# Turning q and k of steps 0 to 5 in TensorE's transpose mode, with half-size loads and with k and v on GpSimd's queue

## The chip, the cores and the metric

The kernel runs on one core of a Trainium2 chip. A core has TensorE (PE, matrix products), VectorE (DVE), ScalarE (ACT), GpSimd (POOL) and SyncE (SP), which run side by side and wait for each other on semaphores. The metric is the device time of one execution in microseconds (us). A measurement is the median of several executions; a profiled execution gives the trace.

## The reference

The program is a retention block followed by a feed-forward block; q, k, v and the result are float32:

```python
# q, k, v: (B=4, H=8, S=768, D=64)
gamma = 1.0 - 2.0 ** (-5.0 - np.arange(H))
for t in range(S):
    state = gamma[None, :, None, None] * state + np.einsum('bhd,bhe->bhde', k[:, :, t], v[:, :, t])
    y[:, :, t] = scale * np.einsum('bhd,bhde->bhe', q[:, :, t], state)
# y as x: 3072 tokens x 512; w_in is 512 x 2048, w_out 2048 x 512
h = x @ w_in
g = h * (1.0 / (1.0 + np.exp(-1.702 * h)))
out = g @ w_out
```

Both weights are float64 and are narrowed to float32 on the chip.

## The kernel before

**Retention by chunks.** The sequence is cut into chunks of 64 positions. A *step* j handles one chunk of two batches at once, the one in partitions 0 to 63, the other in 64 to 127, for all eight heads; there are 24 steps. A step loads q, k and v (`load`), turns q and k so that the head dimension lies in the partitions (`turn`, then `turned` copies the result out of PSUM), multiplies k by q (`attend`, line 288) and masks the product with the decay (`masked`). One step later it takes the state's update from k and v (line 296), the part of the output from the old state (305) and the part from within the chunk (311). `by_state` and `output` join both parts into X, the input of the feed-forward block; `aged` and `updated` bring the state forward, and `decay` scales k for the update.

Steps 0 to 5 (`j < NEW`) and the later ones differ. The early steps load q, k and v as they lie, one DMA for each batch, and turn q and k on TensorE by a matmul with the identity: 16 matmuls a step, each for one head of both batches, with a result of 64 partitions by 128 (line 249). Head `HP * r + s` goes to partitions 64r to 64r+63 of slot s, where HP is 4. ScalarE copies the result out (260) and scales k (271). From step 6 on, VectorE transposes 32 by 32 blocks (252) that were loaded in many small DMAs.

**Feed-forward.** The first block of four steps is multiplied directly (`up0`, line 413), the second too (`up1`, 426); later blocks use fewer products on sums of sub-blocks (471, 575, 708). The weights come in 512 KB transfers (`fetch`, 178) into three raw buffers in turn and are narrowed by ScalarE (`abs`, 205) and VectorE (`half`: 209 to 211, `rest`: 215 to 220).

**What sets the order.** For the opening, one long list of words written by hand gives the order of the work: `k0` loads k of step 0, `turn2` turns step 2, `w3b` fetches half of a weight panel, `abs3 half3 rest3` narrow panel 3, `up0.0.2` is an up-projection, `step-2` is the later half of step 2 and `step3` the first half of step 3. Each engine and each queue executes its own part of the list in this order, and an instruction that waits holds up all those behind it on its engine. The part around the first steps reads:

```python
k0 table q0 warm turn0 w0b rows warm k1 abs0b q1 turned0 step0 v0 w0a half0b mask turn1 causal rest0b
masked0 decay0 v1 decay1 abs0a half0a step-0 updated0 turned1 q2 step1 rowd k2 whole w2b turn2 w2a x0 k3
aged1 masked1 turned2 v2 rest0a abs2 q3 step-1 updated1 state1 decay2 aged2 step2 q4 x1 half2 decay3 w3b
w3a up0.0.0 masked2 turn3 k4 step-2 v3 q5 rest2 k5 gate0.0.0 turned3 updated2 state2 step3 up0.0.2
```

`mask` is a product on VectorE that waits for `rows` on TensorE; `causal` is GpSimd's part of it (772), two instructions that wait for `mask`. `whole` is a pair of small DMAs (783) with the decay over a chunk, which `aged` reads on ScalarE (356). All q, k and v go by SP's queue, except k of step 0, which goes by ScalarE's. The q and k tiles have two buffers each, and so have the v tiles: the load of step j waits until step j - 2 has been read. GpSimd issues only the small decay tables in the opening. `whole_h` (793) is such a table for the steps after 5; it isn't pinned to its place in the list, and the scheduler put it at the head of GpSimd's queue.

Of the kernel before, what the change touches and what calls it, by code (L numbers as in the profile page):

```python
# [11 lines left out]
AF = mybir.ActivationFunctionType  # L12
ALU = mybir.AluOpType
P = 128
# [14 lines left out]
def kernel(  # L29
# [29 lines left out]
    pe, act, dve, pool, sp = nc.tensor, nc.scalar, nc.vector, nc.gpsimd, nc.sync  # L59
    ctx.enter_context(tc.manual_schedule(engines={mybir.EngineType.PE}))  # L60

    B, H, S, D = q.shape
    NT, DM = out.shape
    DFF = moe_w_in.shape[1]
    HP = H // 2
# [38 lines left out]
    cold = const.tile([P, 2 * H], F32, name="cold")  # L104
    whole = const.tile([P, HP], F32, name="whole")
    whole_h = const.tile([P, H], F32, name="whole_h")
    ident = const.tile([P, P], F32, name="ident")
# [10 lines left out]
    def pin(i):  # L118
        return tc.keep_in_program_order(i) if ordered[0] else i


    NEW = 6
    QKV = {}

    def load(j, what="qkv"):

        b, c = j // NC * 2, j % NC
        rows = slice(c * D, (c + 1) * D)  # L130
        keep = tc.keep_in_program_order if j < 2 * CB else lambda i: i

        def plain(name, src, tag, bufs, engine=sp):
            t = two.tile([P, H, D], F32, name=name + "_in", tag=tag, bufs=bufs)
            QKV[name, j] = t
            for i in range(2):
                if j < NEW:
                    keep(engine.dma_start(t[i * D:(i + 1) * D], src[b + i, :, rows, :].rearrange("h p d -> p h d")))  # L138
                else:
                    for r in range(2):  # L140
                        keep(engine.dma_start(t[r * D:(r + 1) * D, i * HP:(i + 1) * HP],
                                              src[b + i, r * HP:(r + 1) * HP, rows, :].rearrange("h p d -> p h d")))

        if j < NEW:
            if "q" in what:
                plain("q", q, "q_sq", 2)
            if "k" in what:
                plain("kn", k, "k_sq", 2, sp if j else act)
        elif "q" in what:
            for name, src in (("q", q), ("k", k)):  # L150
                t = two.tile([P, H, D // C4, C4], F32, name=name + "_sq")
                for r0 in range(0, P, C4):
                    for n in range(D // C4):
                        t0 = c * D + n * C4
                        tc.keep_in_program_order(sp.dma_start(
                            t[r0:r0 + C4, :, n], src[b + r0 // D, :, t0:t0 + C4, r0 % D:r0 % D + C4]
                            .rearrange("h p d -> p h d")))
                QKV[name, j] = t
        if "v" in what:
            if j >= NEW and c < NC - 1:  # L160
                plain("kn", k, "kn", 1)
            plain("v", v, "v", 2)


    w1v = moe_w_in.bitcast(U32).rearrange("(c p) (f two) -> p c f two", p=P, two=2)
# [59 lines left out]
    QT, KT, KD, AT, TURNED, PA, PU, PY, SHARE = [{} for _ in range(9)]  # L225
    HALF = [slice(i * D, (i + 1) * D) for i in range(2)]
    TWO = [(i, r) for i in range(2) for r in range(2)]

    def home(j, name):

        at = ["qT", "kT", "kd", "at"].index(name)
        shape = [[HP, P] if j < NEW else [H, D]] * 2 + [[H, D], [2, HP, D]]
        shape = shape[at]
        if j >= 2 * CB:
            return one.tile([P] + shape, F32, name=name, tag=name, bufs=[2, 1, 1, 2][at])
        t = G[:, at, j % 2 * 2:j % 2 * 2 + 2].rearrange("p s t -> p (s t)")
        return t.rearrange("p (a b c) -> p a b c", a=2, b=HP) if at == 3 else t.rearrange("p (a b) -> p a b", a=shape[0])

    def turn(j):

        QT[j], KT[j] = home(j, "qT"), home(j, "kT")
        if j < NEW:

            x = QKV.pop(("q", j)), QKV["kn", j]
            TURNED[j] = p = [ps.tile([P, HP, P], F32, name="pt", tag="y") for i in range(2)]
            for n in (1, 0) if j else (0, 1):
                for s in range(HP):
                    for r in range(2):
                        pe.matmul(p[n][HALF[r], s, :], x[n][:, HP * r + s, :], ident, start=True, stop=True)  # L249
        else:  # L250
            for t, name in ((QT[j], "q"), (KT[j], "k")):
                tc.keep_in_program_order(dve.transpose(
                    t.rearrange("p h t -> p (h t)"), QKV.pop((name, j)).rearrange("p h n d -> p (h n d)")))
        if 2 * CB <= j < NCH - 2:
            load(j + 2, "qk")
# [6 lines left out]
    def decay(j):  # L262

        if j % NC == NC - 1:
            return
        KD[j] = home(j, "kd")
        x = QKV["kn", j]
        if j < NEW:

            for h in range(H):  # L270
                pin(act.activation(KD[j][:, h], x[:, h], AF.Copy, scale=cold[:, H + h:H + h + 1]))
        else:
            pool.tensor_mul(KD[j].rearrange("p (i s) d -> p i s d", i=2), x.rearrange("p (i s) d -> p i s d", i=2),
                            cold[:, None, H:H + HP, None].to_broadcast([P, 2, HP, D]))
# [94 lines left out]
    def step(j, f=None):  # L369
        attend(j, f)  # L370
        if j is not None:
            masked(j)
            if j > 2 * CB:
                decay(j)
        if f is not None:
            c = f % NC
            if c == 0:
                updated(f)
            else:
                by_state(f)  # L380
            output(f)
            if 0 < c < NC - 1:
                aged(f)
                updated(f)
        if j is not None and 2 * CB < j < NCH - 1:
            load(j + 1, "v")
# [356 lines left out]
    W = col_decay.shape[1]  # L743
# [43 lines left out]
    def late_loads():  # L787
        load(2 * CB, "qkv")
        load(2 * CB + 1, "qk")

    def halves_anew():

        pool.dma_start(whole_h, bass.AP(tensor=col_decay.tensor, offset=col_decay.offset + (D - 1) * W + H,
                                        ap=[[0, P], [1, H]]))
        pool.tensor_copy(mask[HALF[1], 0], mask[HALF[1], 1])
        pool.tensor_copy(cold[HALF[1], H:H + HP], cold[HALF[1], H + HP:2 * H])
        old, new = state[NEW % NC % 2], state[(NEW + 1) % NC % 2]
        for u in range(2):
            pool.dma_start(new[HALF[1 - u], u], old[HALF[u], 1 - u])
        for u in range(2):  # L800
            pool.tensor_copy(old[HALF[u], 1 - u], new[HALF[u], 1 - u])
# [5 lines left out]
        "mask": lambda: pin(dve.tensor_mul(m3, products["rows"], cold[:, 0:H, None].to_broadcast([P, H, D]))),  # L807
        "causal": causal, "rows": rows,
        "rowd": lay_rowd, "whole": lay_whole, "late_loads": late_loads, "anew": halves_anew,
        "warm": keep_warm}  # L810
    for j in range(2 * CB):
        for name in "qkv":
            works[f"{name}{j}"] = lambda j=j, name=name: load(j, name)
        works |= {f"{name}{j}": lambda j=j, do=do: do(j) for name, do in (
            ("turn", turn), ("turned", turned), ("decay", decay), ("masked", masked), ("state", by_state),
            ("x", output), ("aged", aged), ("updated", updated))}
        for f in (None, *range(2 * CB)):
            works[f"step{j}" + ("" if f is None else f"-{f}")] = lambda j=j, f=f: attend(j, f)
        works[f"step-{j}"] = lambda j=j: attend(None, j)
    for i in range(2 * NFF):  # L820
        works[f"w{i // 2}{'ab'[i % 2]}"] = lambda i=i: fetch(i)
    for name, i in [("0a", 0), ("0b", 1)] + [(str(p), 2 * p) for p in range(1, NFF)]:
        n = Narrow(i)
# [41 lines left out]
    for m in range(NB):  # L865
        between = []
        if m == 0:
            between = [lambda: turn(2 * CB), lambda: step(2 * CB), lambda: None, lambda: None, lambda: turn(2 * CB + 1)]
        elif m == 1:
            between = [lambda: (decay(2 * CB), load(2 * CB + 1, "v"))]  # L870
            for j in range(2 * CB + 1, 3 * CB + 1):
                between.append(lambda j=j: (step(j, j - 1), j < 3 * CB and turn(j + 1)))
        elif 1 < m < NB - 1:
            last = min((m + 2) * CB, NCH - 1)
            for j in range((m + 1) * CB + 1, last + 1):
                between.append(lambda j=j: (step(j, j - 1), j < last and turn(j + 1)))
            if last == NCH - 1:
                between.append(lambda: step(None, NCH - 1))
# [77 lines left out]
```

## Time and profile before

| | |
|---|---|
| median of 8 executions | 667.18 us (665.85 to 668.38) |
| profiled execution | 666.63 us, of it 664.9 us from the first to the last instruction (the span) |
| TensorE busy | 649.2 us (98%) |
| VectorE busy | 435.2 us (65%) |
| ScalarE busy | 148.8 us (22%) |
| GpSimd busy | 176.5 us (27%) |
| mean granted TensorE clock | 0.997 |
| line 249, the turns | 192 records, in steps 0 to 5, between 6.6 and 44 us |

How to read it: the rows overlap, as the engines run side by side. Each float32 matmul leaves two records in the trace, so 192 records are 96 matmuls. In the lists that follow, a line gives the engine, the line of the kernel, what is written and read, and a time; `SPq` and `ACTq` are the queues of DMA issues of those engines, while GpSimd's issues are shown as its own instructions. "<-" names what ended a wait.

### The profile page before, as it was taken

What the parts mean: (1) busy time and instruction counts of PE and PEld (TensorE: products, weight loads), DVE (VectorE), ACT (ScalarE), POOL (GpSimd) and SP (SyncE); (2) the same over time, 40 slices, a digit from 0 to 9 for tenths busy, and PEclk for the clock granted to TensorE, in tenths of its full rate; (3) what the DMA queues carried; (4) which work ended last, traced back from release to release, by engine and by line L of the source; (5) the groups of instructions that cost most, each with busy time, mean ns of one, the idle gap of its engine ahead of it and who ended that gap; (6) DMA issues with size and microseconds to landing.
All of it is one profiled execution on the core that took longest, in us unless ns stands there. A gap on an engine that the chain in (4) does not pass through costs nothing.

```text
span 664.9 us, 15234 instructions
## 1 busy us (share of the span) xinstructions
PE 649.2 (98%) x6438; PEld 564.1 (85%) x6438; DVE 435.2 (65%) x618; ACT 148.8 (22%) x285; POOL 176.5 (27%) x196
## 2 busy tenths in 40 slices
PE   6799999999999999999999999999999999999997
PEld 4688885446888888888999888999888999988997
DVE  3789778798545775456985345995254995254965
ACT  5664222231000000233110234010233110233110
POOL 3000310000278326100446500354700255500000
PEclk9899999999999999999999999999999999999999
DMA  9987647542203546263385742285652243602142
GB/s 182 224 205 207 169 83 230 172 80 36 45 12 132 174 108 185 60 226 123 87 221 131 253 90 95 83 203 145 196 155 96 66 147 109 234 20 95 52 157 95
DMA packets 150500, 89.49 MB, mean 135 GB/s; under 512 B 136192, under 2 KB 137472, under 8 KB 149408
## 3 DMA queue, kind: packets, MB, share of 16 engines
q1 hardware_dynamic: 140944, 46.50, 30.4%
q0 software_dynamic: 7184, 40.78, 16.9%
q10 hardware_dynamic: 2304, 1.25, 0.6%
q8 instruction: 50, 0.82, 0.5%
q14 instruction: 18, 0.15, 0.1%
HBM read 72.89 MB, written 15.47 MB: 133 GB/s over the span
## 4 chain that ended last, share of the span: by engine, by line
PE 88%; DMA 4%; DVE 3%; SPq 2%; POOL 2%; issue 1%; ACT 1%; POOLq 0%; DVEq 0%
PE pq L575 24%; PE px L471 16%; PE pd L708 13%; PE py L471 12%; PE ph L426 8%; PE ph L413 5%; PE pa L288 2%; PE py L311 2%; PE pa L296 2%; PE py L305 1%; DMA kn_in<-in_k_dram 1%; PE pt L249 1%; DMA W<-in_moe_w_out_dram 1%; DMA q_in<-in_q_dram 1%; SPq L138 1%
## 5 line engine op out<-in xcount | busy, mean ns | idle before, releaser
L575 PE MATMUL pq<-W,G 128*128 128x128 f32 x672 | 80.5, 276 | 0.5 <-issue 0.5
L575 PEld LDWEIGHTS pq<-W,G 128*128 128x128 f32 x672 | 77.6, 192 | 1.3 <-issue 0.7
L544 POOL DMA_DIRECT2D ring<-W2D x28 | 15.4, 551 | 228.7 <-PE px L471 118.2
L471 PE MATMUL px<-X,W1A 128*128 128x256 f32 x256 | 60.1, 380 | 0.5 <-POOL X L441 0.5
L471 PE MATMUL px<-X,W1B 128*128 128x256 f32 x256 | 59.8, 379 | 0.0
L575 PE MATMUL pq<-ring,own 128*128 128x128 f32 x448 | 59.8, 277 | 0.0
L575 PEld LDWEIGHTS pq<-ring,own 128*128 128x128 f32 x448 | 54.5, 192 | 0.4
L471 PEld LDWEIGHTS px<-X,W1A 128*128 128x128 f32 x256 | 48.3, 190 | 7.5 <-POOL X L441 1.2
L471 PEld LDWEIGHTS px<-X,W1B 128*128 128x128 f32 x256 | 48.6, 190 | 6.6
L708 PE MATMUL pd<-W,G 128*128 128x256 f32 x224 | 49.6, 381 | 0.0
L708 PEld LDWEIGHTS pd<-W,G 128*128 128x128 f32 x224 | 42.3, 190 | 5.8
L471 PE MATMUL py<-X,W1B 128*128 128x256 f32 x192 | 45.4, 379 | 0.0
L471 PE MATMUL py<-X,W1A 128*128 128x256 f32 x192 | 45.4, 379 | 0.0
L392 ACT ACTIVATE G<-G 128x512 f32<-128x512 f32 x48 | 30.2, 630 | 52.0 <-DVE G L481 33.4
L471 PEld LDWEIGHTS py<-X,W1B 128*128 128x128 f32 x192 | 36.5, 190 | 4.9
L471 PEld LDWEIGHTS py<-X,W1A 128*128 128x128 f32 x192 | 36.5, 190 | 4.9
L489 DVE TENSOR_TENSOR t<-py,u 128x512 f32<-128x512 f32 x16 | 11.1, 692 | 32.9 <-PE py L471 32.9
L478 ACT ACTIVATE p<-px 128x512 f32<-128x512 f32 x16 | 9.6, 597 | 94.3 <-PE px L471 94.3
L575 PE MATMUL pq<-ring,G 128*128 128x128 f32 x224 | 29.6, 275 | 0.0
L575 PE MATMUL pq<-W,own 128*128 128x128 f32 x224 | 29.6, 275 | 0.0
L503 DVE TENSOR_TENSOR G<-G 128x512 f32<-128x512 f32 (+2 forms) x24 | 12.3, 514 | 25.7 <-ACT G L392 25.7
L413 PE MATMUL ph<-X,W1B 128*128 128x256 f32 x128 | 29.0, 383 | 0.0
(206 smaller groups left out, 1165.9 us busy)
## 6 DMA issues: line engine op xcount, KB each, us to landing
ring<-W2D POOLq DMA_DIRECT2D x28, 768.0 KB, 4.9
W1B<-W1D POOLq DMA_DIRECT2D x6, 1792.0 KB, 9.1
W<-in_moe_w_in_dram SPq DMA_DIRECT2D x12, 512.0 KB, 6.1
W<-in_moe_w_out_dram SPq DMA_DIRECT2D x10, 512.0 KB, 4.8
out_dram<-o POOLq DMA_DIRECT2D x20, 256.0 KB, 3.2
q_sq<-in_q_dram SPq DMA_DIRECT2D x144, 32.0 KB, 2.2
k_sq<-in_k_dram SPq DMA_DIRECT2D x144, 32.0 KB, 2.3
v_in<-in_v_dram SPq DMA_DIRECT2D x72, 64.0 KB, 3.0
```

What stands on the lines that cost most here:

```text
L288: pe.matmul(pa[HALF[w], u, 0, s, :], kt[HALF[u], w, s, :], qt[HALF[u], w, s, :], start=True, stop=True)
L296: pe.matmul(pa[HALF[u], w, 1, s, :], kd[HALF[w], HP * u + s, :], vn[HALF[w], HP * u + s, :], start=True, stop=True)
L311: pe.matmul(py[HALF[o], w, 0, 2 * u + s2 if f < NEW else 2 * s2 + u, :], vn[HALF[w], HP * u + s, :], a[HALF[w], u, s, :], start=True, stop ...
L392: pin(act.activation(g, h[:, i], AF.Gelu_apprx_sigmoid))
L413: pe.matmul(h[:, ab], w, X[:, 2 * th + c // 2, c % 2, :], start=(ab == 0 and c == 0), stop=(c == 3), skip_group_check=True)
L426: pe.matmul(h, w, X1[:, c // 2:4:2, c % 2, :], start=(c == 0), stop=(c == 3))
L471: pe.matmul(acc[:, u, :], t[:, q1 + u, sa, c, :], X[:, sb, c, :], start=(start and u == 0 and c == 0), stop=(stop and c == 1), skip_group_ ...
L489: dve.tensor_add(tt, z, u)
L503: dve.tensor_sub(q[0][1], q[0][0], q[0][1])
L544: pool.dma_start(c, W2D[i])
L575: pe.matmul(p0[:, j, :], a[:, d], w[:, d], start=(new and j == 0 and d == 0), stop=(d == NP // 2 - 1), skip_group_check=True)
L708: pe.matmul(p0[:, n, :], g1(m, p, sa)[:, n * P:(n + 1) * P], W2[:, sb, p, :], start=(new and p == 0 and n == 0), stop=(last and p == NP - ...
```

## The change

Steps 0 to 5 turn q and k in TensorE's transpose mode, two heads at a time: 8 matmuls a step, each with a result of 128 partitions by 128. For this, heads s and s + 4 must lie side by side, so q and k are loaded in two DMAs for each batch: four heads each, written to every second place. `decay` reads its heads from the new places. k of steps 1 to 5 and v of steps 0 to 5 are issued by GpSimd instead of SP; k of step 0 stays with ScalarE, q with SP. The load of `whole_h` is pinned to its place in the list, and so comes after the last v of these steps on GpSimd's queue.

```diff
             for i in range(2):
                 if j < NEW:
-                    keep(engine.dma_start(t[i * D:(i + 1) * D], src[b + i, :, rows, :].rearrange("h p d -> p h d")))
+                    to, at = t[i * D:(i + 1) * D], src[b + i, :, rows, :].rearrange("h p d -> p h d")
+                    for n in range(1 if name == "v" else 2):
+                        keep(engine.dma_start(*((to, at) if name == "v" else (to[:, n:H:2], at[:, n * HP:(n + 1) * HP]))))
...
-                plain("kn", k, "k_sq", 2, sp if j else act)
+                plain("kn", k, "k_sq", 2, pool if j else act)
...
-            plain("v", v, "v", 2)
+            plain("v", v, "v", 2, pool if j < NEW else sp)
...
                 for s in range(HP):
-                    for r in range(2):
-                        pe.matmul(p[n][HALF[r], s, :], x[n][:, HP * r + s, :], ident, start=True, stop=True)
+                    pe.matmul(p[n][:, s, :], x[n][:, 2 * s:2 * s + 2].rearrange("p r d -> p (r d)"), ident, is_transpose=True)
...
-                pin(act.activation(KD[j][:, h], x[:, h], AF.Copy, scale=cold[:, H + h:H + h + 1]))
+                pin(act.activation(KD[j][:, h], x[:, h % HP * 2 + h // HP], AF.Copy, scale=cold[:, H + h:H + h + 1]))
...
-        pool.dma_start(whole_h, bass.AP(tensor=col_decay.tensor, offset=col_decay.offset + (D - 1) * W + H,
-                                        ap=[[0, P], [1, H]]))
+        pin(pool.dma_start(whole_h, bass.AP(tensor=col_decay.tensor, offset=col_decay.offset + (D - 1) * W + H,
+                                            ap=[[0, P], [1, H]])))
```

## The prediction

> **What bounds the kernel now.** The page comes first: how busy each engine is.
>
> ```profile
> span 664.9 us, 15234 instructions
> PE 649.2 (98%) x6438; PEld 564.1 (85%) x6438; DVE 435.2 (65%) x618; ACT 148.8 (22%) x285; POOL 176.5 (27%) x196
> ```
>
> TensorE idles 15.7 us in all, so time can come only from its own work or from those gaps. The list of its waits says where they lie:
>
> ```profile
> PE idle L762 <- POOL ident masks.py:199: 4.4, 1, 4.4
> PE pt L249 <- DMA kn_in<-in_k_dram: 1.7, 2, 1.4
> PE pa L288 <- DVE state L365: 1.3, 1, 1.3
> PE pa L288 <- ACT W1B L205: 1.1, 1, 1.1
> ...
> PE px L471 <- POOL X L441: 0.5, 1, 0.5
> ```
>
> The longest four end before 53 us. From 95 us to the end TensorE waits 1.3 us altogether; a shift that survives to there arrives at the end, and the whole case is the opening. The chain of waits, cut to the first 110 us, shows how the touched lines stand on it:
>
> ```profile
> 13.23 1.02 SPq L138
> 14.29 5.78 DMA kn_in<-in_k_dram
> 20.21 3.32 PE pt L249 x32
> 23.53 0.87 PE pa L296 x32
> ...
> 30.89 1.90 PE pt L249 x32
> ```
>
> k of step 2 is issued at 13.2, lands at 20.1, and step 2 is turned in 3.32 us at a low clock (granted 0.66 and 0.50 of full in 20 to 24 us, by the table of 2 us windows). Later turns (30.9, 38.7, 42.2) take 1.90 us each and lie wholly on the chain. Last, the timelines of VectorE and TensorE show what stands close behind:
>
> ```profile
> 26.13 0.69 DVE L346 TENSOR_TENSOR X<-py,tmp 128x512 f32<-128x512 f32 x1
> 37.07 0.69 DVE L209 TENSOR_SCALAR W1A<-W1A 128x1024 f32<-128x1024 f32 x1 [1.16 <-ACT W1A L205]
> 42.24 1.23 DVE L220 TENSOR_TENSOR W1A<-W 128x1024 f32<-128x1024 f32 x1
> 44.01 7.17 PE L413 MATMUL ph<-X,W1A 128*128 128x256 f32 x32
> ```
>
> The up-projection at 44.0 needs the weights that VectorE finishes at 43.5: half a microsecond of slack.
>
> **What the skill says.** (1) "TensorE: Matmul & The Clock Gate", Terms: the transpose mode is 4 times faster for FP32. The trace of before has no transpose; its plain FP32 matmuls give the other end, below. Part 4 adds that the mode doesn't count as activity that raises the clock. The low clock near 20 us is there already, and no run yet shows its share. (2) "DMA: Bandwidth & Descriptors", Issuing engines are not separate DMA queues: transfers share the same 16 engines whoever issues them, and another queue saves issue time only. The trace agrees so far: the DMA share is 1.0 or more in every 2 us window from 4 to 24 us. (3) Same page, SWDGE vs HWDGE vs iDMA: GpSimd writes its descriptors to SBUF, where VectorE can lock it out. The trace has a 64x4 copy on GpSimd taking 1.12 us at 49.9 until VectorE's L216 ends, and of the two L799 issues one, under VectorE's L215, of 0.70 against 0.53 us. I allow a few tenths.
>
> **The change, part by part.**
>
> *Turns.* Removed: 96 matmuls (192 records in L249), 1.90 us a step warm, 3.3 to 4.0 us cold. Added: 48 whole-array ones, eight a step. Upper bound: L575 has the same 128x128 by 128 shape in plain FP32, eight records every 0.90 us, so two records and 0.224 us a matmul, 1.79 us a step: nearly nothing saved. Lower bound: a quarter, 0.45 us. I take 0.55 warm and 1.0 cold, saving 1.35 in each of steps 3 to 5 and 2.3 in step 2. Below nothing is excluded warm, as 1.79 is under 1.90.
>
> *SP's queue.* q becomes 4 issues of some 0.61 us (L141's 64 KB median) instead of 2 of 0.64: 1.2 us more a step. Two k and two v issues leave (1.3 us each): 1.4 us less a step in all. The built program gives hardware-queue and software-queue DMAs eight completion semaphores each, so each waits for the landing of the eighth before it. Hence w0b, issued at 2.26, now waits for the first k transfer, about 4.5, and lands near 9.7 instead of 8.4. That delays VectorE's half0b to about 12.0, but mask (which waited for rows until 11.76) ends only 0.3 us later. The later weights move up: w3 stands behind q3 and q4 alone, and should land near 34 instead of 35.8. This spends the 1.16 us wait in the fence above.
>
> *ACT's queue.* k0 is 4 issues instead of 2, about 1.6 us more. The table load slides from 2.5 to 4.1; it is hidden, as ACT waited 4.4 us for w0b. If that cover were gone it would cost 1.6 us.
>
> *GpSimd's queue.* Issue prices are on these rows of the groups by shape and of its timeline:
>
> ```profile
> L685 POOL DMA_DIRECT2D out_dram<-o x8 | 6.0, 750 | 54.9 <-DVE o L684 54.9
> L544 POOL DMA_DIRECT2D ring<-W2D x28 | 15.4, 551 | 228.7 <-PE px L471 118.2
> 12.52 1.84 POOL L772 TENSOR_SCALAR_AFFINE_SELECT mask<-mask 64x512 f32<-64x512 f32 x2 [8.18 <-DVE mask L807]
> 14.31 1.06 POOL L783 DMA_DIRECT2D whole<-in_col_decay_dram  x2
> ```
>
> 128 rows cost 0.55 us, 256 cost 0.75. So a k transfer (256 rows) is 0.75 and a v transfer (512) by the same slope 1.15: 3.0 and 2.3 us a step, 29 us in all, where GpSimd had been idle from 15.4 to 49.9. Bounds: 0.55 each (16 us) and double mine (58 us). whole_h leaves the head (0.57), so ident is ready 0.5 us sooner; TensorE then waits for q0 anyway, so I count nothing. Its new place, after v5, is 30 us ahead of L358, its reader.
>
> What queues behind what decides. k1 and v0 go before causal: about 3.8 to 9.1, inside the 8.2 us that GpSimd waited for mask. causal now runs 12.8 to 14.65, v1 to 16.9, k2 to 19.9, whole to 21.0. Before, k2 went at 13.2 and whole at 14.3. The DMA engines have drained their backlog by about 20 (2 MB of q, k and v at 175 GB/s and 2 MB of weights at 350, from 2.6 us), so k2 lands about 3 us after its issue, near 22.7, and whole near 23.6. Behind whole stand ACT's aged1, then turned2 and abs2:
>
> ```profile
> 20.37 1.28 ACT L356 ACTIVATE state<-state,whole 128x128 f32<-128x128 f32 x4 [2.46 <-DMA whole<-in_col_decay_dram]
> ```
>
> So k2 is 2.6 us later than 20.07. Turn 2 takes it to 23.8, step -1 at the low clock (2.0 to 2.2 us) to 25.9, state1 and x1 (1.4) to 27.2 or, since these waits overlap in part, 27.1; before it was 26.8. **Loss here: 0.3.** aged1 ends at 24.9 and updated1 at 25.6, inside that.
>
> *From x1 to the up-projection at 44.* VectorE was busy 14.7 of these 16.65 us and idle 0.40, 0.39 and 1.16, so it can't finish rest3 sooner than 14.7 after x1. TensorE's own list is 0.36 + 3.65 + 0.55 + 1.56 + 0.5 + 3.65 + 0.55 + 1.56 + 0.55 = 12.9 us after x1 against 17.3 now. VectorE is the later: 14.8 instead of 17.3, **gain 2.5**; 1.9 of TensorE's saving turns into a new wait there. k3 is issued by 24.0, needed near 31.5; v2 26.3 against 32; k4 29.3 against 38; v3 31.6; k5 34.6 against 40: covered by 3 us or more, and a queue at half my speed would eat that.
>
> Sum: 2.5 - 0.3 = 2.2 us; the step at 52.95, which waits for masked4 behind rest1, moves with VectorE. decay reads in another order at the same 0.34 us each: nothing. The profiled execution takes 666.63 (span 664.9 and 1.7 around it): 664.4. The median of the eight is 667.18, 0.55 above that one: **665.0**.
>
> **Rivals.** *B, slower: k2 and whole come late.* If GpSimd's issue costs twice my figure (VectorE's locks, 512-row transfers), v1, k2 and whole end near 27.5, k2 lands at 29 and x1 ends near 33: 6 lost, 2.5 back, 670.7. It decides once k2 lands after about 25. For it: six GpSimd issues now stand between causal and k2, where SP issued directly. Against: 0.53 to 0.78 us in every DMA row of POOL. *C, no change: VectorE or its weights hold.* If w3 lands no sooner, or the clock stays low into up0.0.0 (a microsecond), 1 us or less is left: 666.5. The 0.5 us of slack at 44 speaks for it. That the transpose mode isn't cheaper belongs here: 1.79 us a turn leaves 667 to 668. *D, faster: k2 lands by 21.* Then x1 comes near 25.5 and the gain is 4 to 5: 662.5. For it: the last k2 transfer is half as big. Against: its late issue.
>
> **How the numbers follow.** A measurement of this kernel tells about 0.2% (1.3 us) from no change. Forecast 0.44 (663.2 to 666.4, the upper tail within 0.2%), D 0.13, C 0.18, B 0.25. Faster by over 0.2%: D and most of the forecast, 0.55; within 0.2%: 0.20; slower: 0.25. The range 662.3 to 669.3 leaves out the far ends of D and B.
>
> **What would show it.** In the profile after: L249's successor with half the matmuls and 0.5 to 0.7 us a warm step; k's GpSimd issues at 0.75 and v's at 1.15 us; TensorE waiting for k2 until 22 to 23.5; up0.0.0 starting within a microsecond of 27.5; the up-projection of 44.0 near 41.9 and waiting for VectorE's L220; after 95 us the same rows, about 2 us earlier. I am wrong if k2 comes after 25, if a turn takes over 1.2 us warm, or if TensorE shows new gaps after 60 us.

## The result and the profile after

The changed kernel takes 671.74 us (median of 11 executions, 669.59 to 674.08) against 667.08 for the kernel before beside it (32 executions). The ratio is 1.0068, with a 95% interval of 1.0053 to 1.0083: **slower by 0.7%**, where 665.0 was predicted and 669.3 was the end of the range.

The profiled execution took 672.25 us. The page of the changed kernel, its span and its engine row:

```profile
span 670.6 us, 15000 instructions
PE 646.0 (96%) x6294; PEld 559.9 (83%) x6294; DVE 435.9 (65%) x618; ACT 148.1 (22%) x285; POOL 196.8 (29%) x228
```

TensorE does 3.2 us less work than before, and the span is 5.7 us longer: it idles 24.6 us instead of 15.7. The list of its waits (total, times, longest) says on what:

```profile
PE pt L250 <- DMA kn_in<-in_k_dram: 6.1, 1, 6.1
PE idle L763 <- POOL ident masks.py:199: 3.9, 1, 3.9
PE pa L289 <- DVE G L318: 2.2, 1, 2.2
PE pa L289 <- DVE state L366: 1.9, 1, 1.9
PE px L472 <- POOL X L442: 1.6, 2, 1.4
```

The first line was 1.7 us in two waits; now it is one wait of 6.1, for k of step 2. The chain of waits of the changed kernel, cut to the first 110 us, goes through it (start, length, what):

```profile
14.48 1.32 POOL v_in L140 x2
15.80 1.81 POOL kn_in L140 x3
17.61 7.86 DMA kn_in<-in_k_dram
25.61 1.94 PE pt L250 x8
...
40.23 0.60 SPq L180
40.88 8.12 DMA W<-in_moe_w_in_dram
49.08 1.17 ACT W1A L207
```

GpSimd issues v1, then k2, and k2's data need 7.86 us on the chain. GpSimd's issues themselves, and what waited on ScalarE for `whole`, are in the timeline of the changed kernel:

```profile
14.43 1.37 POOL L140 DMA_DIRECT2D v_in<-in_v_dram  x2
15.78 2.49 POOL L140 DMA_DIRECT2D kn_in<-in_k_dram  x4
18.22 1.12 POOL L784 DMA_DIRECT2D whole<-in_col_decay_dram  x2
25.88 1.28 ACT L357 ACTIVATE state<-state,whole 128x128 f32<-128x128 f32 x4 [7.34 <-DMA whole<-in_col_decay_dram]
```

The four k transfers are issued in 2.49 us (0.62 each) and the two v transfers in 1.37 (0.69 each). Nothing waits for the issuing; the last is out at 18.3, and the data land at 25.5. What changed in front of k2 is on SP's queue. Before, SP issued weight panel 2 behind k2:

```profile
14.98 1.15 SPq L178 DMA_DIRECT2D G<-in_moe_w_in_dram  x2
```

In the changed kernel its first half goes out at 10.95 and its second before v1 and k2 are issued at all:

```profile
12.02 0.37 SPq L180 DMA_DIRECT2D G<-in_moe_w_in_dram  x1
```

Four marks on the way to the end, and the end itself, show where the 5.7 us lie in this execution:

| mark | before | after | later by |
|---|---|---|---|
| turn of step 2 starts | 20.21 | 25.61 | 5.4 |
| x1 (X of step 1) ends | 26.82 | 31.80 | 5.0 |
| third up-projection starts | 44.01 | 46.99 | 3.0 |
| first instruction of `up1` | 103.82 | 107.56 | 3.7 |
| end of the span | 664.9 | 670.6 | 5.7 |

So 5.0 are lost by the end of x1, with k2 late, 2.0 are won between x1 and the third up-projection, 0.7 are lost again before `up1`, and 2.0 after it. Of the last 2.0, 1.1 is the wait for X at L442 (1.6 against 0.5) and 0.4 TensorE's own sequencer; the other 0.5 isn't in the list of waits. The wait for X varies between executions of one kernel (below), and the change edits nothing that runs there. These marks are of one execution. What each part is worth in the median is another question, and the experiments give another answer to it.

### The profile page after: what moved, and what is told of

Its sections match the earlier page's. It is cut to its first block, busy times and chain, and to the rows that moved or that the text cites. A ratio compares the mean times of both kernels' runs of the same rounds, so it can differ in the third digit from the quotient of the medians.

```text
span 670.6 us, 15000 instructions
## 1 busy us (share of the span) xinstructions
PE 646.0 (96%) x6294; PEld 559.9 (83%) x6294; DVE 435.9 (65%) x618; ACT 148.1 (22%) x285; POOL 196.8 (29%) x228
## 4 chain that ended last, share of the span: by engine, by line
PE 79%; DMA 8%; DVE 4%; SPq 4%; POOL 3%; issue 1%; ACT 0%; POOLq 0%; DVEq 0%; ACTq 0%
PE pq L576 21%; PE px L472 16%; PE pd L709 13%; PE py L472 12%; PE ph L427 8%; PE ph L414 4%; DMA kn_in<-in_k_dram 2%; SPq L157 2%; PE pa L289 1%; PE py L312 1%; PE py L306 1%; PE pa L297 1%; DMA W<-in_moe_w_out_dram 1%; SPq L140 1%; DMA W<-in_moe_w_in_dram 1%; DMA k_sq<-in_k_dram 1%
## 5 line engine op out<-in xcount | busy, mean ns | idle before, releaser
L545 POOL DMA_DIRECT2D ring<-W2D x28 | 15.4, 552 | 229.9 <-PE px L472 117.9
L414 PE MATMUL ph<-X,W1A 128*128 128x256 f32 x128 | 29.0, 383 | 0.7 <-DVE X L347 0.7
L504 DVE TENSOR_TENSOR G<-G 128x512 f32<-128x512 f32 (+2 forms) x24 | 12.3, 513 | 25.7 <-ACT G L393 25.7
```

Of the source, the lines that this page charges most:

```text
L414: pe.matmul(h[:, ab], w, X[:, 2 * th + c // 2, c % 2, :], start=(ab == 0 and c == 0), stop=(c == 3), skip_group_check=True)
L504: dve.tensor_sub(q[0][1], q[0][0], q[0][1])
L545: pool.dma_start(c, W2D[i])
```

## Experiments

Two theories stood at first. **Order theory:** k2 lands late because SP's queue, rid of k and v, sends weight panel 2 ahead of k2 or beside it, and GpSimd's transfers get little of the DMA engines meanwhile. **Slow-queue theory:** GpSimd's queue is slow by itself, whatever SP does. In both, half-size loads and the transpose mode have prices of their own. The expectations on record call the order theory W and the slow-queue theory S; H in them says that the half-size loads and the mode are the loss. The first four runs (4 to 6 executions each) take the parts apart.

**e1: all k and v back on SP; half-size loads and transpose mode stay.**

```diff
-                plain("kn", k, "k_sq", 2, pool if j else act)
+                plain("kn", k, "k_sq", 2, sp if j else act)
...
-            plain("v", v, "v", 2, pool if j < NEW else sp)
+            plain("v", v, "v", 2)
```

> As the changed kernel, but k of steps 1 to 5 and v of steps 0 to 5 are issued by SP again, at their old places in the list; transpose mode and half-size loads stay. Theory W (on GpSimd's queue k of step 2 is overtaken by weight panel 2, which SP now issues 4 us before it): k2 stands ahead of w2 again and lands near 20 to 21, the clock stays up, and only the cheaper turns are left: 664 to 666.5. Rival H (the half-size loads and the transpose mode are the loss, not the queue): 670 or more, with k2 still landing after 23.

Measured: 672.52 against 667.58, ratio 1.0079 (1.0059 to 1.0099). k2 is turned at 22.1, but SP now has ten issues a step and the weights come late: ScalarE waits 5.58 us for panel 3 and 5.34 for panel 1, and `up1` starts at 110.2. So half-size loads can't simply go back to SP. Neither expectation holds as stated: the time is Rival H's, the landing of k2 isn't.

**e2: the queues alone** (the kernel before, whole loads and plain turns, with k of steps 1 to 5 and v on GpSimd, and `whole_h` in its new place).

```diff
-                plain("kn", k, "k_sq", 2, sp if j else act)
+                plain("kn", k, "k_sq", 2, pool if j else act)
...
-            plain("v", v, "v", 2)
+            plain("v", v, "v", 2, pool if j < NEW else sp)
```

> As the kernel before, with plain turns and whole-size loads, but k of steps 1 to 5 and v of steps 0 to 5 on GpSimd's queue and the whole_h load pinned. Theory W: k2 lands near 25 as in the changed kernel and the turns save nothing: 672 to 674. Rival H: the queue costs nothing, 666 to 668.

Measured: 672.92, ratio 1.0094 (1.0075 to 1.0112). k2 is issued by 17.7 and turned at 23.4. The queues alone cost 5.3 us, no less than the whole change, as Theory W had it; k2 comes 1.6 us sooner than it said.

**e3: the changed kernel with weight panel 2 behind q3 in SP's list.**

```diff
-        rowd k2 whole w2b turn2 w2a x0 k3
+        rowd k2 whole turn2 x0 k3
...
-        v2 rest0a abs2 q3 step-1
+        v2 rest0a q3 w2b w2a abs2 step-1
```

> As the changed kernel, but weight panel 2 is issued after q of step 3 on SP's queue instead of before it, so some 7 us later; nothing else moves. Theory W: the DMA engines are free for v1 and k2, k2 lands near 21 to 22 and whole near 22.5, x1 of step 1 ends 2 to 3 us sooner than in the changed kernel, less what the later panel 2 costs: 667 to 670. Rival S (GpSimd's queue is slow by itself, whatever stands beside it): k2 lands at 24.5 or later and the time is 671 to 674, as panel 2 comes later too.

Measured: 672.26, ratio 1.0076 (1.0055 to 1.0098). The panel moves from 11 to 18.1, but k2's issue moves too (to 19.3), so the two still meet, and k2 is turned at 25.7. Both figures are those that Rival S expected; but as the panel went out beside k2 after all, the run doesn't tell the theories apart.

**e4: half-size loads alone** (the change with k and v on SP and with plain turns, 16 matmuls a step; `whole_h` stays in its new place).

```diff
-                    pe.matmul(p[n][:, s, :], x[n][:, 2 * s:2 * s + 2].rearrange("p r d -> p (r d)"), ident, is_transpose=True)
+                    for r in range(2):
+                        pe.matmul(p[n][HALF[r], s, :], x[n][:, 2 * s + r, :], ident, start=True, stop=True)
```

> As the kernel before in its queues and with plain matmuls for the turns, but q and k in the half-size loads of the changed kernel. It shows the price of the half-size loads alone, and against the run with the old queues and transpose mode the worth of the mode alone. Theory W: SP issues 2.5 us more a step, of which the idle DMA engines after 24 us hide most: 666.5 to 669. Rival H: 670 or more.

Measured: 675.99, ratio 1.0133 (1.0114 to 1.0151): the half-size loads on SP cost 8.4 us, so on this queue Rival H is right about them. e4 and e1 differ by the mode alone: it saves 3.5 us. The queues alone (e2) stand at 1.0094, the half-size loads with the mode on SP (e1) at 1.0079, and all of it together at 1.0068: the prices don't add up, since each move relieves what the other burdens.

The next four tell the two theories apart: two keep weight panel 2 off SP's queue while k2 moves, and two put k or v back.

**f1: the changed kernel, weight panel 2 issued by GpSimd behind k2 and `whole`.**

```diff
-        pin(sp.dma_start(x.rearrange("p (c f) two -> p c f two", c=2) if i < NFF else x, SRC[i]))
+        pin((pool if i in (4, 5) else sp).dma_start(x.rearrange("p (c f) two -> p c f two", c=2) if i < NFF else x, SRC[i]))
```

> As the changed kernel, but weight panel 2 is issued by GpSimd, right behind whole, so that in one queue it stands behind v1, k2 and whole and can't overtake them. Theory W (transfers of weights that enter the DMA engines ahead of k2 hold it up; GpSimd's queue itself is as fast as SP's): k2 lands 3 us sooner than in the changed kernel, at 22 to 22.5, and x1 of step 1 ends near 28.5 instead of 31.8; panel 2, later now, takes part of that back: 667.5 to 670.5. Rival S (k2 lands 7 us after its issue whatever else runs): k2 at 25 or later, 671 to 674.

Measured: 671.15 against 667.67, ratio 1.0050 (1.0034 to 1.0065), with runs from 667.03 to 674.66. The profile is of the fastest of them. In it k2 is issued by 17.5, as in the changed kernel (18.3), and turned at 20.8 instead of 25.6. k2 lands even sooner than Theory W had it, but the time falls in Rival S's range.

**f2: v back on SP, `whole` moved ahead, weight panel 2 behind q3.**

```diff
-        rows warm k1 abs0b
+        rows warm k1 whole abs0b
...
-        rowd k2 whole w2b turn2 w2a x0 k3
+        rowd k2 turn2 x0 k3
...
-        v2 rest0a abs2 q3 step-1
+        v2 rest0a q3 w2b w2a abs2 step-1
```

> A version drawn from the runs so far: transpose mode and half-size loads as in the changed kernel, k on GpSimd's queue and v back on SP's, so that SP issues no more a step than in the kernel before and GpSimd's k2 stands right behind causal; whole goes ahead of causal, weight panel 2 behind q of step 3. Theory W: k2 issued near 14.5 to 17 with less ahead of it lands near 21, the turns are a microsecond cheaper each, and the time is 663 to 667. Rival S: k2 at 23.5 or later, 669 or more.

Measured: 669.88, ratio 1.0037 (1.0023 to 1.0051). k2 is issued by 16.5, turned at 20.6, and the first up-projection starts at 24.7, 2.4 us before that of the kernel before. But weight panel 2 is issued only at 21.75, ScalarE waits 7.7 us for it, and `up1` starts at 108.0, so the expected 663 to 667 isn't reached.

**f3: the changed kernel with v back on SP.**

```diff
-            plain("v", v, "v", 2, pool if j < NEW else sp)
+            plain("v", v, "v", 2)
```

> As the changed kernel with v of steps 0 to 5 back on SP's queue; k stays on GpSimd's. k2 is issued 1.4 us sooner, as v1 no longer stands ahead of it, and v0 and v1 on SP's queue push weight panel 2 back by 2.6 us. Theory W: both help k2, which lands near 22.5 to 23.5: 668 to 670.5. Rival S: only the 1.4 us: 671 to 672.5.

Measured: 668.52, ratio 1.0016 (1.0004 to 1.0028). SP issues weight panel 2 at 16.2 to 17.3; k2 is issued by 17.5 and turned at 24.7, later than Theory W had it, and yet the time is in its range.

**f4: the changed kernel with k back on SP, v on GpSimd.**

```diff
-                plain("kn", k, "k_sq", 2, pool if j else act)
+                plain("kn", k, "k_sq", 2, sp if j else act)
```

> As the changed kernel with k of steps 1 to 5 back on SP's queue; v stays on GpSimd's. SP has 8 issues a step (5.1 us) against 6 (3.9) before and 10 with all on it. Theory W, with the second half that the earlier runs showed (SP's issue time delays the weights behind it): between the two runs with all on SP and all moved, k2 near 20.5 to 21.5, weights 1 and 3 1 to 2 us late: 668 to 671. Rival S (only the issue count of SP matters, not what overtakes what): 671 to 673.

Measured: 669.74, ratio 1.0035 (1.0019 to 1.0051). k2 goes by SP until 16.6, the panel right behind it, and k2 is turned at 21.3 (the profiled execution took 667.25, below the median).

**The verdict on the two theories.** In all these runs, and in those that follow, k2's delay goes by where weight panel 2 is, not by the queue that carries k2:

| kernel | k2's queue | weight panel 2 | last issue of k2 | turn of step 2 starts |
|---|---|---|---|---|
| before | SP | SP, behind k2 | 14.9 | 20.2 |
| f4 | SP | SP, behind k2 | 16.6 | 21.3 |
| after | GpSimd | SP, before k2 (10.95) | 18.3 | 25.6 |
| after, once more | GpSimd | SP, before k2 | 18.0 | 23.8 |
| e2 | GpSimd | SP, before k2 (9.36) | 17.7 | 23.4 |
| e3 | GpSimd | SP, beside k2 (18.1) | 19.3 | 25.7 |
| f3 | GpSimd | SP, beside k2 (16.2) | 17.5 | 24.7 |
| f1 | GpSimd | GpSimd, behind k2 | 17.5 | 20.8 |
| f1, once more | GpSimd | GpSimd, behind k2 | 17.7 | 20.6 |
| g2 | GpSimd | GpSimd, behind k2 | 17.1 | 20.5 |
| g2, once more | GpSimd | GpSimd, behind k2 | 16.6 | 20.7 |
| f2 | GpSimd | SP, long after (21.75) | 16.5 | 20.6 |

With SP's panel before or beside it, 5.7 to 7.3 us pass from k2's last issue to the turn; without it, 2.9 to 4.1 on the same queue (in h1 and h3 below 4.0, in h2 2.6). The slow-queue theory falls. The DMA view of the window from 16 to 18 us shows what goes with it (queue, packets, MB, share of the 16 engines' time; q1 is SP's queue, q0 GpSimd's). The changed kernel, with k2 and v1 outstanding on q0:

```profile
DMA packets 366, 0.71 MB, mean 357 GB/s; under 512 B 24, under 2 KB 24, under 8 KB 366
q1 hardware_dynamic: 360, 0.69, 101.6%
q0 software_dynamic: 6, 0.02, 3.5%
```

The same window of f1's second profile, with the panel not yet issued:

```profile
q0 software_dynamic: 115, 0.28, 50.3%
q1 hardware_dynamic: 243, 0.06, 13.1%
```

While the panel's packets pass (0.69 MB, some 2 KB each), GpSimd's queue moves 0.02 MB; without them it moves 0.28. The Trainium skill's page "DMA: Bandwidth & Descriptors", Queues, rings and completion order, has each engine take turns between the queues it has work for, packet by packet. Six packets against 360, with k2 and v1 issued and waiting, don't look like turns; whether a packet of this view is what that page calls a packet isn't shown. The measurement decides here; what holds GpSimd's packets back stays open.

Windows of 0.5 us show how sharp it is. In the changed kernel GpSimd's queue moves no packet from the issue of v1 (14.43) to 17.5, in its second profile none from 14.11 to 16.5, in e2 none from 15.0 to 17.5; each time the first packets come when those of the panel get fewer. In both profiles of f1 they come within 1.7 us of the issue, although VectorE runs the same instructions there (L211 to L213 and L366), so VectorE's work doesn't tell the two apart. The starving isn't the whole delay: from its first packets to k2's landing GpSimd's queue needs 7 to 8 us in the two profiles of the changed kernel and 5 to 6 in those of f1, for the same v1 and k2. Why it is slower after the panel too isn't shown.

**What the table leaves over.** f1 restores k2 and still stands at 671.15, while f3, with a late k2, stands at 668.52. v on GpSimd must have a price that isn't k2's landing. The next four runs look for it, and for a version without the loss.

**g1: steps 0 to 2 as before (whole loads, plain turns, SP's queue); steps 3 to 5 with half-size loads, the mode and k on GpSimd; all v on SP.**

```diff
-                    for n in range(1 if name == "v" else 2):
+                    for n in range(1 if name == "v" or j < 3 else 2):
...
-                plain("kn", k, "k_sq", 2, pool if j else act)
+                plain("kn", k, "k_sq", 2, pool if j > 2 else sp if j else act)
...
-            plain("v", v, "v", 2, pool if j < NEW else sp)
+            plain("v", v, "v", 2)
```

(The turn and `decay` follow the same condition.)

> Steps 0 to 2 keep whole loads, plain FP32 turns and SP's queue; steps 3 to 5 alone have half-size loads, transpose mode and k by GpSimd; q and v stay on SP. Theory (what costs is k2 on GpSimd's queue beside weight panel 2 on SP's): k2 is back in SP's order and lands near 22 as before, weight panel 2 is issued behind it near 15, the first up-projection stands near 27.2, three turns are 1.0 us shorter each and the net of SP's list is one k (two DMAs) less and one q half (two DMAs) more per step: up1 starts near 102 to 104, the time is 665 to 667.5. Rival (half-size loads cost by themselves, wherever they stand, by pushing weights late): w1 or w3 still wait over 3 us, up1 near 106, 669 or more.

Measured: 668.84 against 667.74, ratio 1.0013 (0.9996 to 1.0030): between the two expectations. k2 is turned at 20.0, panel 3 makes ScalarE wait only 1.1, but `up1` starts at 106.2. TensorE has a gap of 2.9 us at 34 in front of line 316 for which the profile names no releaser, so this one is left unexplained.

**g2: f1 with v back on SP** (k and weight panel 2 on GpSimd).

> The changed kernel with v of steps 1 to 5 back on SP and weight panel 2 (its two DMAs) issued by GpSimd behind k2. Theory (two separate costs: k2 late because SP's weight packets stand beside it, and v on GpSimd): k2 lands within 4 us of its last issue, near 21, TensorE's clock does not drop before step 2, up1 starts near 103 to 104, and the runs lie closer together than with v on GpSimd: 665 to 667.5. Rival (the moved weight panel costs again what the early k2 saves, as where it was moved before, whose median was 671.15): 669 to 671.

Measured: 666.47 against 667.74, ratio 0.9980 (0.9963 to 0.9996). k2 is turned at 20.5; `up1` starts at 104.3.

**f1 and the changed kernel once more, for second profiles.**

> The kernel with weight panel 2 on GpSimd behind k2 once more, for a second profile. Its first profile was of its fastest run (667.03 against a median of 671.15). If k2's landing makes its spread, a run near 671 shows k2 landing after 23 us or the clock at half speed before step 2; if not, k2 lands near 21 again and the time goes later, between 27 and 107 us.

> The changed kernel as it is, for a second profile. Theory: k2 lands 6 to 7.5 us after its last issue, near 25, with SP's weight packets in the engines from 14 to 18; up1 starts near 107. Rival (the late landing is an accident of one run): k2 lands within 4 us, near 22.

Measured (one execution each): f1 took 671.6. k2 is turned at 20.6 and the clock is full until 36: k2 is **not** what makes f1 slow. What is late is weight panel 2, issued at 18.7 and there at 26.8 (24.8 in the first profile), with ScalarE and VectorE in order behind it. k5 is late too: it is issued until 38.4, its turn waits for it until 45.7, and the third up-projection starts at 46.6 instead of 42.2. The changed kernel took 670.87, with k2's turn at 23.8 and `up1` at 106.8: the late landing repeats, by 5.8 us instead of 7.3.

**h1, h2, h3 and g2 once more: which v costs?** h1 is f1 with v1 behind `whole`, so that k2 goes first. h2 and h3 are g2 with v of steps 3 to 5, or of steps 0 to 2, on GpSimd.

```diff
# h1
-        masked0 decay0 v1 decay1
+        masked0 decay0 decay1
...
-        rowd k2 whole w2b
+        rowd k2 whole v1 w2b
# h2
-            plain("v", v, "v", 2)
+            plain("v", v, "v", 2, pool if 2 < j < NEW else sp)
# h3
-            plain("v", v, "v", 2)
+            plain("v", v, "v", 2, pool if j < 3 else sp)
```

> All v on GpSimd as in the changed kernel, weight panel 2 on GpSimd, but v1 issued behind k2 and whole instead of ahead of them. If v costs by its place ahead of k2, k2 is issued about 1.4 us earlier, lands near 20, and most of the 4.7 us between 671.15 and 666.47 comes back: 667 to 668.5. If it costs by the late steps, the time stays at 670 to 671.5.

> The best kernel so far (k and weight panel 2 on GpSimd, v on SP, 666.47) with v of steps 3 to 5 alone put on GpSimd. If the late v are what costs (their issue waits for a buffer and holds k behind it; they move beside SP's panels), 669 to 671, with k4 or k5 late at their turns. If the early v are, 666 to 667.5.

> The best kernel so far (666.47) with v of steps 0 to 2 alone put on GpSimd, ahead of k2 and weight panel 2. If the early v are what costs, weight panel 2 lands after 25.5 and the time is 669 to 671. If the late v are, 666 to 667.5.

> The best kernel so far once more, beside these: k2 lands near 20.5, up1 starts near 103 to 104.5, 665.5 to 667.5 and below the kernel before by 0.1 to 0.3%. If its first result was chance, it stands at or above the kernel before.

Measured beside a kernel before of 667.19: h1 670.07, ratio 1.0044 (1.0029 to 1.0060), and in its profile, of its slowest execution (677.51), k2 is issued no earlier (15.4 to 18.0, as GpSimd first waits for its part of the mask); h2 669.63, 1.0033 (1.0016 to 1.0051); h3 667.30, 1.0006 (0.9988 to 1.0023); g2 667.31, 1.0000 (0.9985 to 1.0015). The early v cost nothing that can be measured in the median, though three of h3's 14 executions took over 670, and its profile is of one of these; **v of steps 3 to 5 on GpSimd cost 2.3 us**. And g2 doesn't repeat its 0.998: it is as fast as the kernel before, not faster. No version here beats it for certain.

Why the late v cost in h2 is much the same story once more. In g2's second profile GpSimd has issued k5 by 34.5. In h2 the two v3 issues (1.37 us) stand ahead of k5, and its second half waits another 1.08 us until a transfer of k4 has landed, by GpSimd's timeline:

```profile
35.66 1.47 POOL L140 DMA_DIRECT2D kn_in<-in_k_dram  x2 [1.08 <-DMA kn_in<-in_k_dram]
```

So k5 goes out only until 37.1. By then SP has issued panels 1 and 5 (35.0 to 37.2). The chain of h2 and its DMA view from 38 to 40 us:

```profile
36.27 8.43 DMA kn_in<-in_k_dram
```

```profile
q1 hardware_dynamic: 333, 0.58, 104.8%
q0 software_dynamic: 3, 0.00, 1.3%
```

GpSimd's queue gets 3 packets in 2 us beside SP's 333, and k5 needs 8.4 us on the chain. Step 5 is turned at 44.8, in g2's second profile at 41.6: k5 is starved there too (14 packets in the same window), but was issued 2.6 us earlier. f1's second profile and h1's show the same wait inside k5's issues (1.6 and 2.3 us) and a late k5.

**What each part is worth in the median.** Four kernels differ in two things alone, the queue of v and the queue of weight panel 2 (ratios to the kernel before beside each):

| | panel 2 on SP | panel 2 on GpSimd, behind k2 |
|---|---|---|
| v on GpSimd | 1.0068 (the changed kernel) | 1.0050 (f1) |
| v on SP | 1.0016 (f3) | 1.0000 and 0.9980 (g2, twice) |

Taking v back is worth 0.5% or more (3.3 us and up) in both columns. Moving the panel behind k2, which brings k2 in 3 to 5 us sooner, is worth about 0.2% (1.2 us) in both rows if g2's second result is taken (0.4% with its first); 0.2% is no more than the noise of such a difference. So most of what k2 loses in one execution's marks is made up later, and the larger part of the 0.7% is v's. How v costs in the changed kernel itself isn't shown: there k5 comes in time, and step 5 is turned at 45.88 without a wait.

## Why the prediction was wrong, step by step

**The step that failed** is "the DMA engines have drained their backlog by about 20 [...] so k2 lands about 3 us after its issue, near 22.7". k2 landed at 25.5, 7.2 us after its last issue and 2.8 later than forecast. The 3 us are not absurd: f1 and g2 have them when no weight panel of SP's stands in the way. The prediction moved k and v off SP's queue and saw that "the later weights move up", but worked that out for panel 3 alone. Panel 2 moved too, from 14.98 (behind k2) to 10.95 (in front of it). The one queue had kept k2 ahead of the panel; two queues didn't. The fault lies in treating 2 MB of q, k and v and 2 MB of weights as one backlog that serves all alike. This step is what moved the mark at x1; in the median it is the smaller part of the loss (the table of the four kernels).

**A term put at nothing.** For the later transfers on GpSimd's queue the prediction wrote "covered by 3 us or more" and counted no cost. Taking v off that queue is worth 3.3 us or more, the larger part of the loss. h2, f1 and h1 show one way in which it costs, k5 issued late and then starved; in the changed kernel's own profiles k5 is in time, so the way there stays open.

**Rival B was on the right side for a wrong reason.** It gave 670.7 with "k2 lands after about 25" as its point of decision, and k2 landed at 25.5. But its mechanism, GpSimd's issue at twice the figure, is false. Issue took less than forecast: 0.62 us a k transfer against 0.75, 0.69 a v transfer against 1.15. (Its lower bound was summed wrongly: 32 issues at 0.55 us are 17.6 us, not 16; nothing rests on it.) The warning from the skill's "DMA: Bandwidth & Descriptors", SWDGE vs HWDGE vs iDMA, of which a few tenths were allowed, shows no cost in these rows.

**What the other queue brings.** The skill's statement that another queue saves issue time only ("Issuing engines are not separate DMA queues") was cited for what another queue can gain. The runs show the other side: it can cost (e2, the queues alone, 5.3 us). Panel 2 went out before k2 instead of behind it, and GpSimd's queue starved beside it.

**The turn.** 0.55 us was taken warm. A warm turn of the changed kernel, from its timeline (a group's length includes the end of its last matmul; the step's next work starts at 36.38):

```profile
35.41 0.60 PE L250 MATMUL pt<-ident,kn_in 128*128 128x128 f32 x4
35.85 0.60 PE L250 MATMUL pt<-ident,q_in 128*128 128x128 f32 x4
```

Four follow each other in 0.44 us, 0.11 each; the chain has 0.89 for the turn, against 1.90 before: 1.0 us saved, not 1.35. A plain FP32 matmul of this shape was 0.224 by the prediction's own row, so the mode is twice as fast as that row, not the four times of the skill's "TensorE: Matmul & The Clock Gate", Terms. The text had named that as one bound and took a value close to it; e4 against e1 gives 3.5 us for the mode in all.

**From x1 to the third up-projection** 14.8 us were forecast instead of 17.3. It is 15.2 in the changed kernel, a gain of 2.0 where 2.5 was forecast: this step held. g2's first profile shows it with k2 in time. Its timeline of TensorE and its chain:

```profile
41.89 7.17 PE L414 MATMUL ph<-X,W1A 128*128 128x256 f32 x32
48.99 0.69 PE L289 MATMUL pa<-G 64*64 64x64 f32 x32
51.87 0.69 PE L289 MATMUL pa<-G 64*64 64x64 f32 x32 [2.18 <-DVE G L318]
...
54.66 5.61 PE L414 MATMUL ph<-X,W1A 128*128 128x256 f32 x21
```

```profile
34.63 9.29 DMA W<-in_moe_w_in_dram
44.01 1.16 ACT W1A L207
...
51.12 0.61 DVE G L318
```

The up-projection starts at 41.89, just where the prediction put it ("near 41.9"). **But the gain doesn't live.** "[T]he step at 52.95 [...] moves with VectorE" is the second step that failed: that VectorE work waits for weight panel 1, whose DMA takes 9.3 us, so the step comes at 51.87, 1.1 earlier and not 2.1. TensorE waits 2.18 us for it. The kernel before already waited for that panel, on ScalarE, as its timeline shows; the prediction took the step for VectorE's alone:

```profile
45.10 1.15 ACT L205 ACTIVATE W1A<-W 128x1024 f32<-128x1024 f32 x1 [1.92 <-DMA W<-in_moe_w_in_dram]
```

TensorE's clock is then down (0.73, 0.50 and 0.91 in the 2 us windows from 52 to 58), and the next up-projection starts at 54.66 against 54.98 before. Of 2.1 us, 0.3 is left, and `up1` starts at 104.3 against 103.8. g2's second profile ends in the same place with the clock full throughout: up-projection at 43.19, the step at 52.62, the next up-projection at 54.65, `up1` at 103.3. So the late panel caps the gain without a low clock as well. In the changed kernel the same wait (2.19 us, at 56.98) stretches the way from the third up-projection to the fourth from 11.0 us to 12.0. This is why the best version only draws level.

**The low clock** added nothing to the loss by x1 against the kernel before. It was at 0.50 from 22 to 30 us, longer than before, and ate most of what the mode saves in the turn of step 2 (1.94 us instead of 3.32): from that turn's start to the end of x1 it is 6.2 us, against 6.6 before. The 5.0 us at x1 are the late k2.

**After 95 us** "the same rows, about 2 us earlier" came 3.7 later, and another 2.0 were added, 1.5 of them in waits. The wait for X at L442 is 1.6 us here, 0.9 in the second profile, 0.7 and 2.1 in the two of f1, 0.2 and 2.0 in the two of g2. It doesn't follow the edits, and why it varies stays open, as do f1's wide spread beyond its late panel and k5, and g1's gap.

## What to carry to other kernels

When loads leave a shared queue, list what moves up on the queue they leave: a large transfer that stood behind them may now stand in front, and the landing time of the small ones can follow from that more than from their issue price. Check it in the DMA view by queue, in windows of 2 us: a queue with issued transfers and hardly a packet is being starved. Don't read the cost off the first late mark: vary each moved load by itself and compare medians, as a delay at one mark may be made up before the end. And here a microsecond saved on TensorE lasted only as far as the next weight panel: look for the next DMA wait on the chain before adding up gains.

## What was not expected of the hardware

- Beside SP's weight packets GpSimd's queue moved 6 packets against 360, and 3 against 333, in 2 us. Free of them, it landed 256 KB of k about 3 us after the last issue (f1, g2).
- GpSimd issued 64 KB transfers of 256 rows in 0.62 us each, and 128 KB transfers of 512 rows in 0.69: the price hardly goes with the rows. SP's price is the same for 64 and 128 KB (0.60 to 0.65 us), so halving the transfers doubles the queue's time; e4, which does only that, is 8.4 us slower.
- The transpose mode leaves one record a matmul in the trace where a plain FP32 matmul leaves two: 48 records in the turns where there were 192.
